# Folding landmark sums with shifted copies and VectorE additions, and loading the first k through SyncE, in a Nystrom attention plus feed-forward kernel

## The chip, the cores and the metric

The kernel runs on one core of a Trainium2 chip. The metric is device time in microseconds (us): the median of 12 runs before the change is 254.02 us, from 252.98 to 255.0. A core has five engines: TensorE (PE, matrix products; PEld is its weight load), VectorE (DVE), ScalarE (ACT), GpSimd (POOL) and SyncE (SP). They run their own instruction streams in order and meet through semaphores. SBUF is the on-chip memory with 128 partitions; PSUM holds what TensorE writes, in eight banks. Loads and stores are issued by SyncE or GpSimd and carried by 16 DMA engines.

## The reference

The reference is a Nystrom approximation of attention for 8 batches of 8 heads (576 tokens, 64 values a head), and a feed-forward layer on its output.

```python
q_lm = q.reshape(B, H, m, S // m, D).mean(axis=3)      # m = 32 landmarks, 18 tokens each
k_lm = k.reshape(B, H, m, S // m, D).mean(axis=3)
A  = sm(q, k_lm); Bm = sm(q_lm, k_lm); C = sm(q_lm, k) # softmax of scaled products
Z  = Bm.T / (norm1(Bm) * norminf(Bm) + 1e-6)
for _ in range(6):
    Z = 2 * Z - Z @ Bm @ Z                             # approximate inverse of Bm
attn = A @ Z @ C @ v                                   # per batch and head
h = attn_rows @ w_in                                   # 512 -> 2048
out = (relu(h) ** 2) @ w_out                           # 2048 -> 512
```

## The kernel before

**Attention.** For each batch, q and k are brought into a transposed form (`Ts`) in which a partition holds one of 64 values of a head for one of two parities of a token pair: partitions 0 to 63 the one, 64 to 127 the other. A landmark is a sum over 18 tokens. Summing along the free axis gives one partial sum for each parity (`parts["k"]` is the tile `kpart`, `parts["q"]` lies in `qpad`). The two parities must still be added. A *fold* does this on PE (line 681): a 128x128 matrix of four identity blocks times the partial sums puts into each half of the partitions the sum of both. For k the result is copied from PSUM into `kdup` (one copy of 128 x 256, line 686); for q into a block-diagonal tile `bdq` (two copies of 64 x 256, line 690). These copies go through the helper at lines 388 (ACT) and 390 (DVE).

`kdup` and the landmarks of q give the landmark scores (`b_mm`, lines 704 and 707); from them come the softmax and the inverse iteration, a chain of small steps that passes between PE and DVE (lines 869, 882 and 532 for the later batches; 732, 739 and 769 for batch 0). `bdq` and the transposed k give the scores C (line 917), whose exponentials (`EC`, line 924, ACT) are multiplied with v (lines 948 and 966). The product, normalised, meets the inverse (`Z4T`, `u`, `WT`), and `WT` times w_in gives `G` (line 1061). The softmaxed A is `AT`.

**Feed-forward.** `mlp_in` multiplies `AT` with `G` (line 1123 and the helper at 380), ACT takes the relu (1135), DVE squares it into `gT` (1138). `mlp_out` multiplies `gT` with w_out, 128 rows at a time, 16 matmuls of 512 columns each (1179); the result is copied from PSUM and stored by SyncE (1151), two pieces a tile. The very last tile is done in two cuts of columns, 0 to 256 and 256 to 512, each with its own copy and its own two stores.

**Batches.** The attention of batch b+1 is prepared while the feed-forward of batch b runs. Batches 0 and 1 get q and k in their transposed form by transposes on PE, with the landmark sums made on PE as well (lines 620, 630, 634); batches 2 to 7 get it by DMA transposes (548), and DVE sums (665, 668, 672).

**The order of the work.** Nothing runs in program order. Every operation is added to a plan (`Plan.add`) with the engine or engines that may do it, an assumed duration, what it reads and writes, the PSUM banks that it needs and a priority. `Plan.schedule` is a list scheduler: it takes the operation that can start earliest by its own model, critical ones first, then by priority. The choice between ACT and DVE for a copy (`either`) is made there too. The model has constants for latencies, for the DMA rate and for the delivery of PE's instructions in blocks of 256 (`BLOCK`, `AHEAD`, `FETCH`; idle warm-up matmuls and others count as `words`). `SHIFTS` is a packed table with one byte for each operation, which moves its priority, and `LOADS` does the same by hand for a few loads: in this kernel it exchanges v of batch 0 with the first quarter of w_in, and q with k of batch 1.

**The start.** SyncE loads heads 0 to 3 of k of batch 0 as float32 into the tile `kst`; ACT and DVE cast them into `kraw`, two heads each. GpSimd issues, in this order: the other half of k, both halves of q (these loads cast to bfloat16 on the way), the constants (`seg`, `ident`, `ones_f`), the first quarter of w_in, v, the second quarter of w_in, then q and k of batch 1, the rest of w_in and w_out. Meanwhile PE does 46 matmuls on zeros.

Of the kernel before, what the change touches and what calls it, by code (L numbers as in the profile page):

```python
# [9 lines left out]
P = 128  # L10
AF = mybir.ActivationFunctionType
ALU = mybir.AluOpType
# [3 lines left out]
F32 = mybir.dt.float32  # L16
# [18 lines left out]
LOADS = {11: 1.0, 12: -1.0, 14: 1.0, 15: -1.0, 20: 2.0, 22: -2.0}  # L35
SHIFTS = (
    "_kifEfPk#i`q#~XfPjF2fPjF2fPjFBw0!LK=GcTw3xm*acD7r)u|3E|?W>i|#1YHMcY%OszY04YG&)mLh+-9>?AvdR3UC<^KPWP&Mg0m*l0h"
    "_%bZcA%ZD+H0i~lW7WuJ&lPTK6G=)s#-*XVSf=zA4wOST1cgQj|u(lT}wNDPZtbZMf}#}gaUJs9OFG1t|~P}x1Of-_=LNTlOU#Fu&BK-ZgUn"
    "T$APhO|v`S3?L=76_~Y4F?~P6Df{V1EuXy4|%j;l_xzh0T@jMBZ&b4Fdri~B_9a^A2$I=JPIL5!)Y<Q69LhK4x5Sp0k^QE2R{J>RIy1aBr60"
    "EQqX6y41DQRp=tkZifyGII5;#z=XX7Bp1zTrkYmFhTqR=thl~G=%F5l1onpw>@ax+DYvuC))$H@w#PId9ykXkJaefgG;WOlWLk}ger@_<My7"  # L40
    "Hy+*z>ZQ{{Hs=^YAHFjFE4spYb+acmITS^T7Ux{(p@2I8C4S;_0{BbLjv2?ZE%Q$Bym4se<#6&yPRcMP9n8qm|KxE!#qTR4x@GMvGpp|H?z>"
    "FsX<CY0l7DZ+{wN7{YvU3W6(Fo+c(NbXnC%S0>IT@tn;Yl!`+-Z61DVUX>(Oaw2t7VJMIt(%j^>vH1A-&O9=<wvI@#lKlKX-~Ii;|0nnHs*C"
    "Sr)bY|^vEfE>>A<_q$J&9^)dlFYHS^HM=G@O~lZW@&^iaz3=dnx1@<0IrbDK7}v3xB)HAo6z0R|<s20-OLP5}=e8!Cfl1Trr^1b;0t1Tr`c4"
    "+P*lHdI^;SOh%;K}Q4xGztU-QxO_&#Va6^9SQ~0SKR^Gx>o7;b3GdfQch4(eoA1D7^(9~n>2euUgR7g6_*qgNCTcB6ee*o5vO?)lq(<sr~&M"
    "S7IFe;;<)$LKr7T7cM-k`Ty_nY2!ApE-mFM=;BEnncY4pNcUWjf1T_JmIs`&up3`6ax+DJsgyHpK<Il{VV7eTWX{@;G0sT#*(YjI8osh*NPW"
    "k%mxEN9{EgeD(KRY@wC|J$(K_3Ji0Z1(Y4hb7>511V$L;(doS1mLTPi`Af!YLjWtRy!90ZTMjO(z2u6sVPsHVBe5859@<J17knF989l0Rcl7"
    "z=#9~dIt~%SzVVvL|K;%lKjy~lbfg{QA|}&3Qm-aD=P`Q6wnPTy01u1j;?(L5WoKwKoAfi1hxe%0ggK$b#^d$R%Hh^Q9F#km~=K!0%jZn0#C"
    "AhjsX{7CLztImKO^dZ5{>;Rx@~+Bs+pe|0>OHz;W|Ul6aPMFCcj<1S_YFDg4c|>t?YS8Vu8bDFLK%I*$%~7h&^&ZX`2UgaQ-HBVPdl0gOddl"
    "%@n16bMngR0&i}WBXz#I2tFPLE5#N`u#TLrCi*C4e)jIJ7&3?g5|nwBGGz58mKRqATD`MK9%fdzmuMy#dBbIp#_-|cg%R|sD^@3X*pwp!f_N"
# [10 lines left out]

class Op:
    __slots__ = ("idx", "eng", "fn", "deps", "prio", "acq", "keys", "dma", "end", "grp", "fin", "mode",
                 "crit", "lead", "words", "pre", "fill")


class Plan:
# [1201 lines left out]
```

The softmax here doesn't subtract the row's maximum and nothing guards it: scores larger than these inputs give would overflow.

## Time and profile before

| what | value |
|---|---|
| median of 12 runs | 254.02 us |
| the profiled execution, its own time | 254.07 us |
| its span, first to last instruction | 252.4 us |
| PE busy | 243.3 us (96%) |
| DVE busy | 173.0 us (69%) |
| ACT busy | 164.5 us (65%) |
| fold matmuls (L681) | 16, two a batch |
| landing of k's SyncE half / GpSimd half | 5.0 / 7.6 us |
| landing of q's first / second half (batch 0) | 9.2 / 10.5 us |
| landing of w_in's first quarter / v (batch 0) | 13.3 / 16.9 us |
| first feed-forward matmul (L1123) | 24.1 us |
| last matmul ends / span ends | 248.5 / 252.4 us |

The span is counted from the first to the last instruction of the core; the rest of the execution's own time lies around it. In the rows of the profile, "L1179 PE" is line 1179 on TensorE. A row of a group of instructions gives the total busy time, the mean of one in ns, and after the bar the idle time of the engine ahead of them with what ended it. The chain that ended last is followed back from the last instruction to what released each step; its rows are start and length. "issue" is time in which an engine waited for nothing that the profile shows. Matmuls are pipelined, so the mean length of one (a latency) is longer than the distance from one to the next. In the DMA rows, a load that casts to bfloat16 is counted by the bytes that it writes, half of those that it reads.

### The profile page before, as it was taken

Reading aid. Unit: us, or ns where it says so; the run is one execution under the profiler, and the core shown is the slowest. Engines: PE = TensorE matmul, PEld = TensorE weight load, DVE = VectorE, ACT = ScalarE, POOL = GpSimd, SP = SyncE. Lnnn points to the kernel's source line nnn. Section 1 sums busy time; section 2 is a strip of 40 time slices with the busy share of each in tenths; the row PEclk is TensorE's granted clock in tenths of the full one; section 3 lists DMA queues with packets and bytes.
Section 4 is the critical chain, followed back from the end, with each engine's and each line's share of the span. In section 5 each row is a group of like instructions: output and inputs, shape, how many; then the busy total and the mean of one; then the engine's idle time right before and its main releaser. Section 6 shows DMA issues by size and latency. Waiting matters only on the chain.

```text
span 252.4 us, 6542 instructions
## 1 busy us (share of the span) xinstructions
PE 243.3 (96%) x2658; PEld 144.3 (57%) x2658; DVE 173.0 (69%) x479; ACT 164.5 (65%) x287; POOL 28.3 (11%) x51
## 2 busy tenths in 40 slices
PE   7787999999999999999999999999999999999993
PEld 7563874457654665466546565656554664466453
DVE  4655787869874999499699797987932756477000
ACT  3385998068773997388779987667814873388021
POOL 7822200003003000300210003001000000000000
PEclk9997999999999999999999999999999999999998
DMA  7999999999989999799599678999122203211123
GB/s 136 187 208 205 204 207 205 195 182 159 209 170 168 175 189 172 118 214 166 117 159 248 125 152 118 212 174 180 55 61 73 71 6 86 60 35 32 42 83 87
DMA packets 57055, 35.59 MB, mean 141 GB/s; under 512 B 29760, under 2 KB 52544, under 8 KB 57024
## 3 DMA queue, kind: packets, MB, share of 16 engines
q0 software_dynamic: 22672, 18.06, 47.9%
q1 hardware_dynamic: 34352, 17.11, 32.0%
q8 instruction: 21, 0.34, 0.5%
q14 instruction: 10, 0.08, 0.1%
HBM read 36.70 MB, written 9.44 MB: 183 GB/s over the span
## 4 chain that ended last, share of the span: by engine, by line
PE 90%; DMA 4%; POOL 2%; issue 1%; DVE 1%; ACT 0%; POOLq 0%; DVEq 0%
PE ps L1179 50%; PE ps L380 15%; PE ps L1123 13%; DMA vraw<-in_v_dram 4%; PE ps L1061 4%; PE ps L917 2%; PE ps L966 1%; PE ps L869 1%; PE ps L899 1%; PE ps L1006 1%; PE ps L681 1%; PE ps L707 1%; POOL qraw L456 1%; PE ps L948 0%; PE ps L560 0%
## 5 line engine op out<-in xcount | busy, mean ns | idle before, releaser
L1179 PE MATMUL ps<-w_out_bf,gT 128*128 128x512 bf16 (+1 forms) x592 | 144.8, 374 | 0.0
L1135 ACT ACTIVATE r<-ps 128x576 bf16<-128x576 f32 x128 | 76.3, 659 | 11.8 <-PE ps L380 10.2
L1179 PEld LDWEIGHTS <-gT 128*128 128x128 bf16 x592 | 53.5, 98 | 46.2 <-issue 5.7
L1138 DVE TENSOR_TENSOR gT<-r 128x576 bf16<-128x576 bf16 x128 | 55.7, 451 | 17.5 <-PE ps L1179 8.6
L1123 PE MATMUL ps<-AT,G 128*128 128x288 bf16 x256 | 66.3, 288 | 0.0
L380 PE MATMUL ps<-AT,G 128*128 128x288 bf16 x256 | 66.2, 287 | 0.0
L388 ACT COPY o<-ps 128x512 f32<-128x512 f32 (+1 forms) x30 | 17.0, 571 | 42.0 <-PE ps L1179 40.6
L380 PEld LDWEIGHTS <-G 128*128 128x128 bf16 x256 | 25.1, 98 | 10.6 <-issue 0.2
L1123 PEld LDWEIGHTS <-G 128*128 128x128 bf16 x256 | 25.1, 98 | 9.9 <-ACT G L388 0.8
L388 ACT CAST G<-ps 128x1024 bf16<-128x1024 f32 (+2 forms) x22 | 19.5, 939 | 5.6 <-PE ps L1061 5.5
L390 DVE CAST G<-ps 128x1024 bf16<-128x1024 f32 (+2 forms) x14 | 14.9, 1069 | 8.8 <-PE ps L1061 8.7
L882 DVE SCALAR_TENSOR_TENSOR st<-st,ps 128x128 bf16<-128x128 bf16 x35 | 9.9, 284 | 10.8 <-PE ps L869 10.8
L553 POOL COPY gate<-qT 1x1 bf16<-1x1 bf16 x6 | 1.2, 194 | 126.5 <-DMA qT<-qraw 107.2
L924 ACT ACTIVATE EC<-ps 96x512 bf16<-96x512 f32 x24 | 13.3, 604 | 0.5 <-PE ps L917 0.5
L869 PEld LDWEIGHTS <-Pd 128*128 128x128 bf16 x84 | 7.8, 97 | 8.5 <-DVE Pd L532 1.7
L532 DVE TENSOR_TENSOR Pd<-st,ones_d 128x256 bf16<-128x256 bf16 x42 | 12.1, 288 | 0.9
L1011 ACT ACTIVATE Ra<-ps 128x576 f32<-128x576 f32 x16 | 10.3, 652 | 3.5 <-PE ps L380 3.3
L1022 DVE TENSOR_TENSOR AT<-Ea,Ra 128x576 bf16<-128x576 bf16 x16 | 11.8, 751 | 0.3 <-ACT Ra L1015 0.3
L999 ACT ACTIVATE Ea<-ps 128x576 bf16<-128x576 f32 x16 | 9.8, 650 | 2.6 <-PE ps L899 2.6
L1061 PE MATMUL ps<-w_in_bf,WT 64*32 64x512 bf16 (+1 forms) x264 | 10.6, 390 | 0.0
L560 PE MATMUL ps<-zeros 128*128 128x128 bf16 (+2 forms) x52 | 6.8, 298 | 2.2 <-DVE zeros L482 1.3
L917 PEld LDWEIGHTS <-kT 128*128 128x128 bf16 x192 | 7.3, 98 | 2.6 <-issue 0.7
(156 smaller groups left out, 247.7 us busy)
## 6 DMA issues: line engine op xcount, KB each, us to landing
vraw<-in_v_dram POOLq DMA_DIRECT2D x8, 576.0 KB, 7.5
out_dram<-o SPq DMA_DIRECT2D x23, 192.0 KB, 2.6
qraw<-in_q_dram POOLq DMA_DIRECT2D x7, 576.0 KB, 13.3
kraw<-in_k_dram POOLq DMA_DIRECT2D x7, 576.0 KB, 11.1
out_dram<-o SPq DMA_DIRECT2D x24, 128.0 KB, 2.5
w_in_bf<-in_moe_w_in_dram POOLq DMA_DIRECT2D x4, 512.0 KB, 15.2
w_out_bf<-in_moe_w_out_dram POOLq DMA_DIRECT2D x4, 512.0 KB, 21.3
out_dram<-o SPq DMA_DIRECT2D x23, 64.0 KB, 2.3
```

Of the source, the lines that this page charges most:

```text
L380: nc.tensor.add_instruction(mybir.InstMatmult(start_tensor_calc=start, stop_tensor_calc=stop, is_transpose=transpose, ldweights=False, til ...
L388: nc.scalar.copy(dst, src)
L390: ENG[e].tensor_copy(dst, src)
L532: nc.vector.tensor_tensor(dst[:], src.unsqueeze(2).to_broadcast([P, 2, NG, M]), ones_d[:].unsqueeze(1).to_broadcast([P, 2, NG, M]), ALU.mult)
L917: nc.tensor.matmul(t[:, y, :], lhsT=Ts["k"][z][:, o:o + P], rhs=flat(bdq[:, h, :, :]), start=True, stop=True)
L924: nc.scalar.activation(EC[:, x, :, :, :, :].rearrange("p c i g m -> p (i g) c m"), PS[sc][0:TP, :, :].rearrange("p y (c m) -> p y c m", c= ...
L1022: add(("DVE", dve_ns(S)), lambda e, i=i: nc.vector.tensor_tensor(AT[:, i, :], Ea[:, i, :, :].rearrange("p c t -> p (c t)"), Ra[:, i, :, :] ...
L1061: nc.tensor.matmul(ts[i][M * g:M * g + M, lo:hi], lhsT=WT[64 * i:64 * i + 64, g, :], rhs=w_in_bf[64 * i:64 * i + 64, g, n * 512 + lo:n * 5 ...
L1123: (again if j else nc.tensor.matmul)(t[:, j, 0:HALF], lhsT=G[:, i, f * P:(f + 1) * P], rhs=AT[:, i, j * HALF:(j + 1) * HALF], start=(i == ...
L1135: add(("ACT", act_ns(S)), lambda e, hk=hk, r=r: nc.scalar.activation(r.rearrange("p (j t) -> p j t", j=2), PS[hk][:, :, 0:HALF], AF.Relu), ...
L1138: add(("DVE", dve_ns(S, 2)), lambda e, r=r, f=f: nc.vector.tensor_tensor(gT[:, f, z * S:z * S + S], r[:], r[:], ALU.mult), reads=[("r", rn ...
L1179: nc.tensor.matmul(PS[ok][:, 0:hi - lo], lhsT=gT[:, f, x0:x0 + P], rhs=w_out_bf[:, f, lo:hi], start=(f == f0), stop=(f == f1 - 1))
```

## The change

Four things are changed, and the table of shifts is a new one.

1. For batches 2 to 7 (`b > FOLD`) the fold matmul and the copies from PSUM go. The partial sums are copied into a second tile (`swaps`) with the two halves of the partitions exchanged, by two copies of 64 partitions on ACT or DVE, and DVE adds the two tiles: one addition into `kdup`, two of 64 partitions each into `bdq`.
2. All of k of batch 0 is loaded by SyncE as float32, in four loads of two heads, and cast by eight copies of one head each. Its transposes on PE run in four groups of six instead of two of twelve, with up to three filler matmuls each where PE would wait. GpSimd issues the first half of q, makes the constants, then issues the second half of q.
3. `LOADS` now exchanges the two parts of w_out in each pair, and no longer v with w_in, nor q with k. v of batch 0 is issued ahead of w_in.
4. The last tile is cut at column 384 in place of 256.

The planner's constants (DMA rate, time to landing, durations of issues, instruction delivery) are changed as well; they act on the order alone.

```diff
-LOADS = {11: 1.0, 12: -1.0, 14: 1.0, 15: -1.0, 20: 2.0, 22: -2.0}
+FOLD = 1
+LOADS = {26: 1.0, 27: -1.0, 29: 1.0, 30: -1.0}
...
-    DMA_NS_PER_BYTE = 1.0 / 410.0
+    DMA_NS_PER_BYTE = 1.0 / 401.0
...
-    BLOCK, AHEAD, FETCH = 256, 67, ((20000.0, 6000.0), (165000.0, 6800.0), (1e12, 4000.0))
+    BLOCK, AHEAD, FETCH = 256, 67, ((22000.0, 6400.0), (165000.0, 6800.0), (1e12, 4000.0))
...
-        dma_free = 2900.0
+        dma_free = 2150.0
...
+    swaps = {nm: sb.tile([P, NG, 2, M], BF16, name=nm + "sw") for nm in ("k", "q")}
...
-    kst = sb.tile([TP, H // 2, NC6 * D], F32, name="kst")
+    kst = sb.tile([TP, H, NC6 * D], F32, name="kst")
...
+            fine = not first or nm == "k"
...
-                n = 12 if first else 6
-                tag = "h" if first else "o"
+                n = 6 if fine else 12
+                tag = "o" if fine else "h"
...
+                        if n == 6:
+                            idle(bank(tp, [P, 512]))
...
+            if b > FOLD:
+
+                for x in range(2):
+                    add(either(256, 4), lambda e, x=x, part=parts[nm], sw=swaps[nm]: copy(
+                        e, sw[64 * x:64 * x + 64], part[64 - 64 * x:P - 64 * x]),
+                        reads=[(nm, "part", 0), (nm, "part", 1)], writes=[(nm, "sw", x)], prio=at(pk))
+                if nm == "k":
+                    add(("DVE", dve_ns(256, 2)), lambda e: nc.vector.tensor_tensor(
+                        kdup.rearrange("p (g i) m -> p g i m", i=2), parts["k"][:], swaps["k"][:], ALU.add),
+                        reads=[("k", "part", 0), ("k", "part", 1), ("k", "sw", 0), ("k", "sw", 1)], writes=["kdup"], prio=at(pk))
+                else:
+                    for i in range(2):
+                        r = slice(64 * i, 64 * i + 64)
+                        add(("DVE", dve_ns(256, 2)), lambda e, i=i, r=r: nc.vector.tensor_tensor(
+                            bdq[r, :, i, :].rearrange("p (g i) m -> p g i m", i=2), parts["q"][r], swaps["q"][r], ALU.add),
+                            reads=[("q", "part", 0), ("q", "part", 1), ("q", "sw", i)], writes=["bdq%d" % i],
+                            prio=at(pk + 0.05))
+                continue
...
-            cuts = [(0, 256), (256, 512)] if last else [(0, 512)]
+            cuts = [(0, 384), (384, 512)] if last else [(0, 512)]
...
-    def stage_k(e):
-        nc.sync.dma_start(kst.rearrange("p h (c d) -> p h c d", c=NC6),
-                          k[0, 0:H // 2].rearrange("h (p c) d -> p h c d", c=NC6))
-
-    add(("SP", 60.0), stage_k, writes=["kst"], dma=4.0 * (H // 2) * S * D, prio=-200.0, lead=1250.0)
-    load("k", 0, 2, (1,))
-    for x in range(2):
-        add(either(2 * NC6 * D), lambda e, x=x: copy(
-            e, raws["k"][0][:, 2 * x:2 * x + 2].rearrange("p h c d -> p h (c d)"), kst[:, 2 * x:2 * x + 2, :]),
-            reads=["kst"], writes=[("k", 0, 0, x)], prio=-100.0)
-    load("q", 0, 2)
+    for g in range(NG):
+        def stage_k(e, g=g):
+            nc.sync.dma_start(kst[:, 2 * g:2 * g + 2].rearrange("p h (c d) -> p h c d", c=NC6),
+                              k[0, 2 * g:2 * g + 2].rearrange("h (p c) d -> p h c d", c=NC6))
+
+        add(("SP", 500.0), stage_k, writes=[("kst", g)], dma=4.0 * 2 * S * D * 1.07, prio=-200.0 + g, lead=900.0,
+            land=520.0)
+        for x in range(2):
+            add(either(NC6 * D), lambda e, h=2 * g + x: copy(
+                e, raws["k"][0][:, h].rearrange("p c d -> p (c d)"), kst[:, h, :]),
+                reads=[("kst", g)], writes=[("k", 0, g, x)], prio=-100.0 + g)
+
+    def load_q(x):
+        hs = slice(4 * x, 4 * x + 4)
+        add(("POOL", 670.0), lambda e: nc.gpsimd.dma_start(
+            raws["q"][0][:, hs], q[0, hs].rearrange("h (p c) d -> p h c d", c=NC6)),
+            writes=[("q", 0, x)], dma=4.0 * 4 * S * D * 1.08, prio=ld(), lead=1300.0 - 500.0 * x, land=1150.0)
+
+    load_q(0)
     add(("POOL", 2200.0), constants, writes=["ident", "seg", "onesf"], prio=ld())
+    load_q(1)
```

## The prediction

> **What bounds the kernel now.** I read the page's busy times first, then the stage windows, then the chain that ended last, and for the two ends of the span the queues and the time line.
>
> ```profile
> span 252.4 us, 6542 instructions
> PE 243.3 (96%) x2658; PEld 144.3 (57%) x2658; DVE 173.0 (69%) x479; ACT 164.5 (65%) x287; POOL 28.3 (11%) x51
> ...
> 20.00:25.00 5.00, 4.22 (x61) 1.65 (x60) 2.60 (x6) 2.50 (x7) 1.37 (x2) 0.69 1.31 208
> ...
> 60.00:200.00 140.00, 139.88 (x1453) 80.88 (x1451) 110.31 (x295) 101.57 (x174) 10.93 (x18) 1.00 0.88 152
> ```
>
> The columns of a window are its length, then busy time of PE, weight loads, DVE, ACT and POOL, the granted clock, DMA share and GB/s. From 60 to 200 PE is never idle and DVE has 29.7 us free: there time is saved only by taking work off PE. From 20 to 25 the granted clock is 0.69.
>
> ```profile
> 6.52 10.42 DMA vraw<-in_v_dram
> 16.98 1.19 PE ps L948 x24
> ...
> 19.48 0.24 DVE Z4T L983
> ...
> 20.48 0.78 issue
> 21.25 0.19 PE ps L732 x3
> ```
>
> This is the chain (start, length): the start of the program, up to the first feed-forward matmul at 24.1, hangs on the landing of v at 16.94, then on small steps, then on 0.78 us in which PE has nothing to issue. Afterwards it is PE back to back until the last matmul ends at 248.53; 3.9 us of copy, store and closing follow.
>
> ```profile
> DMA packets 120, 0.18 MB, mean 369 GB/s; under 512 B 0, under 2 KB 120, under 8 KB 120
> ...
> q1 hardware_dynamic: 120, 0.18, 108.6%
> DMA packets 205, 0.15 MB, mean 151 GB/s; under 512 B 9, under 2 KB 205, under 8 KB 205
> ...
> q0 software_dynamic: 205, 0.15, 137.1%
> ```
>
> The DMA answers for 3 to 3.5 us (the SyncE load of half of k, f32 into f32) and 5 to 6 us (GpSimd loads, which write bf16, so 151 written is 302 read). The SyncE load moves its bytes faster than the GpSimd loads beside it.
>
> **1. No fold on PE for batches 2 to 7.** Twelve matmuls at L681 go. First a piece of the chain, then rows of groups (busy us, mean ns | idle before).
>
> ```profile
> 32.94 0.22 PE ps L681 x2
> ...
> L681 PE MATMUL ps<-kpart,fold 128*128 128x256 bf16 x8 | 2.2, 272 | 0.0
> L681 PE MATMUL ps<-qpad,fold 128*128 128x256 bf16 x8 | 2.2, 274 | 0.0
> L532 DVE TENSOR_TENSOR Pd<-st,ones_d 128x256 bf16<-128x256 bf16 x42 | 12.1, 288 | 0.9
> L390 DVE CAST kdup<-ps 128x256 bf16<-128x256 f32 x4 | 1.7, 419 | 0.9 <-PE ps L681 0.9
> ```
>
> The chain piece gives the pitch: two in 0.22 us, 0.11 each (272 is latency). 12 x 0.11 = -1.3 us, in stages where PE is the limit. It is 0 if PE waits in the freed slots, and little more than 1.3 at best.
>
> In exchange the copies of the folded sums from PSUM go. In these six batches DVE did three of kdup (0.42) and five of bdq (0.42), 3.4 us; ACT did three (0.39) and seven (0.37), 3.7 us. Added are 18 additions of 256 bf16 on DVE: by the L532 row, the same operation at that size, 0.288 each, 5.2 us. Added too are 24 shifted copies of 256 bf16 on 64 partitions, on either engine. No row has this form. The bounds are 0.19 (the 64-element cast at L826, 191 ns) and 0.42 (the PSUM cast); between them the 3072-element v copy (941 ns at L958) scales to about 0.22 on DVE if a fixed 0.15 is taken off first. I take 0.22 on DVE, or 0.37 on ACT. All on DVE: 5.2 + 5.3 - 3.4 = +7.1 us on DVE, -3.7 on ACT. All on ACT: +1.8 on DVE, +5.2 on ACT. I cost it at nothing: 7.1 us lie inside DVE's 29.7 idle and beside the previous batch's output matmuls. Without that cover it is up to +7.1. The adds wait for both copies, so behind them in DVE's order the squares into gT and the inverse iteration's steps wait; PE's weight loads wait for these now only 1.7 us (Pd) and 0.9 us (gT) in total.
>
> **2. The start.** All of k(0), four SyncE loads of two heads, replaces one SyncE load of four heads and a GpSimd load of the rest. Three SyncE issues are added (0.38 us each by the one at 0.81) and one GpSimd issue of 0.80 goes. SyncE has nothing else queued there. GpSimd now issues q's first half, makes the constants (2.31 us, 3.48 to 5.79 before), then issues q's second half.
>
> *Bytes.* Before, half of k was in by about 4.3 and q's last byte by about 9.9 (landing 10.5): 1.77 MB read in 5.6 us. After: 0.59 MB of k at 369 GB/s, 1.6 us, and 1.18 MB of q at about 0.36 MB/us read (the 7 to 10 us rows write 176 to 184 GB/s), 3.3 us: 4.9 us, or -0.7. At the 0.30 of the 5 to 6 us row it is -0.1; at the later 0.41 (w_in parts landing 2.5 us apart) -1.1. I take -0.7, the rate of the nearest time.
>
> The Trainium skill (DMA: Bandwidth & Descriptors, "Issuing engines are not separate DMA queues") speaks against this term: DMAs from any engine interleave on the same 16 DMA engines, and spreading them saves only sequencer issue time. By it this term is 0 and the sum ends 0.7 higher.
>
> *q's second half is issued later:* 4.35 in place of 2.82. The first GpSimd packet came about 2.4 us after its issue (1.37 to after 3.5), so these come by 6.8, when k and q's first half still fill the engines (to 7.5 at these rates). So 0; +1.5 if paid whole.
>
> *v goes ahead of w_in's first part* (the old order table exchanged them, the new one doesn't). v then lands at 9.2 + 2.9 + 0.65 = 12.7, not 16.94. Next late is the exponential of the scores, EC, done at 15.90: v's wait is worth up to 16.94 - 15.90 = 1.04. But the time line has a second gate. PE stalls on issue at 14.48 to 15.06 and 20.48 to 21.25, 6.2 us apart, and single 16 KB packets of the instruction queue start at 12.65, 18.85 and after 24.5, also 6.2 apart: PE's program comes in blocks, and arriving early only lengthens the second stall. Blocks move only as far as the words ahead of them are issued sooner, which follows k and q. I take half, -0.5 (ends 0 and -1.04, and -1.82 with the 0.78 stall gone too).
>
> The skill's Runtime: NRT & Kernel Launch, "Instruction fetch mechanics", has fetches in 16 KB blocks too, but calls the cost of a crossing mostly hidden. The trace's 0.78 us stall disagrees; by the rule v would be worth the whole 1.04, and the sum would end 0.5 lower.
>
> *Other edits here.* k's transposes in four groups of six: the 46 warm-up matmuls hold PE until 5.7 either way, so the first group gains nothing. The eight casts of 384 elements (two of 768 took 0.83 and 0.59) and two more kT copies run while ACT and DVE are idle: 0, at most +0.3 if the last cast is exposed. Up to nine filler matmuls run only where PE waits: 0, though their words use up blocks. w_in's first part lands near 15.3, ahead of its use at 23.1. The later parts, 1.6 to 1.9 us ahead of their use now, come 0.7 earlier for a use 1.2 earlier: about 1.1 of cover left, else that is the loss. w_out is reordered: its third part, now last, lands near 42.6 for a use near 43.4.
>
> Start together: -0.7 - 0.5 = -1.2 us (ends -2.5 and, with the late q, +0.8).
>
> **3. The end.** The last tile is cut at 384 in place of 256. PE does the same columns. The last copy shrinks from 0.37 to about 0.27 us. But the first cut's copy now ends some 0.35 us before the last matmul, not 1.35 before it, and SyncE issues four stores in a row:
>
> ```profile
> 247.20 1.80 SPq L1151 DMA_DIRECT2D out_dram<-o  x2
> ...
> 249.09 0.84 SPq L1151 DMA_DIRECT2D out_dram<-o  x2
> ```
>
> One at 0.53 and one at 1.22 in the first pair. With issues of 0.53 the last pair starts about 0.2 later after the last matmul than now; with a 1.22 again, 0.9. A gain is at most 0.1. I take +0.2.
>
> **4. The new order.** The table of shifts and the planner's constants give another order everywhere. No row prices it. In the chain after 30 us little but PE is listed, so it can give back at most about 1 us; a loss is bounded by nothing but the slack above. I take 0 and widen by 1.
>
> **Sum.** 254.07 (the profiled execution: span 252.4 and 1.67 around it; 0.05 above the median of 254.02) - 1.3 - 1.2 + 0.2 = 251.8 us; alone, this case spans 250.9 to 252.7.
>
> **Rivals.**
> - *The start gains it all* (250.5): the blocks move with the data, -2.5 in place of -1.2. For it: 1.04 plus 0.78 stand on the chain. Against: the fixed 6.2 us. 0.15.
> - *The start gains nothing* (253.0): same engines, same bytes, same blocks. For it: the 302 GB/s row. 0.15.
> - *Nor does the fold* (254.3): its slots turn into waits. For it: the freed 0.11 us slots are scattered. Against: no idle PE to hide in. 0.09.
> - *q's late issue is paid whole* (253.8): 254.07 - 1.3 + 0.8 + 0.2. Against: the DMA engines are busy then. 0.05.
> - *DVE becomes the bound* (slower): the additions stand ahead of the gT squares and the inverse iteration in batches 2 to 7. If half of the 7.1 us shows on PE, 251.8 + 3.55 = 255.4. It decides from about 3.0 us, 0.5 a batch (251.8 to 254.8). For it: DVE is 79% busy from 60 to 200 and in-order. Against: 29.7 us idle, and PE has output matmuls to do meanwhile. 0.17.
>
> **How the numbers follow.** The forecast has 0.39. A measurement of this kernel tells about 0.3%, 0.76 us, from no change. Faster holds the forecast and the first two rivals, 0.69; same the next two, 0.14; slower the last, 0.17. The range, 250.0 to 255.0, leaves out the far part of the slower case and the lowest part of the first rival, under 0.2 together.
>
> **What would show it.** L681 down to 4 matmuls; PE still full from 60 to 200, with DVE nearer 84% than 79%; waits of PE's weight loads on Pd and gT not above 3 us. v landing near 12.7 and no longer on the chain; q's second half landing near 9.8; the first feed-forward matmul (L1123) near 22.9 in place of 24.1; issue stalls still about 6.2 us apart. About 4.1 us from the last matmul to the end of the span. I am wrong if q's second half lands after 10.5, if the first block comes no earlier, or if PE shows gaps behind DVE after 60 us.

## The result: 255.75 us, 0.7% slower

The changed kernel takes 255.75 us (median of 12 runs, 254.23 to 256.46); the kernel before, on the same chip, 253.61. The ratio is 1.0072, with a 95% interval of 1.0049 to 1.0095. The forecast was 251.8 and the range ended at 255.0: wrong in its sign and outside its range.

The profiled execution took 255.71 us, with a span of 253.8 (254.07 and 252.4 before). Cut at the two events that the prediction used, the two profiled executions compare as follows.

| | before | after | difference | predicted |
|---|---|---|---|---|
| first feed-forward matmul | 24.11 | 26.25 | +2.14 | -1.2 |
| from it to the end of the last matmul | 224.41 | 223.58 | -0.83 | -1.3 |
| from there to the end of the span | 3.88 | 3.97 | +0.09 | +0.2 |
| around the span | 1.67 | 1.91 | +0.24 | 0 |

The sum is +1.64. The loss stands in the first 26 us.

### The profile after

The page's head, and stage windows (length, then busy time of PE, weight loads, DVE, ACT and POOL, the granted clock, DMA share, GB/s):

```profile
span 253.8 us, 6549 instructions
PE 244.8 (96%) x2648; PEld 143.9 (57%) x2648; DVE 178.5 (70%) x508; ACT 165.9 (65%) x290; POOL 27.6 (11%) x50
...
10.00:15.00 5.00, 4.62 (x82) 4.24 (x83) 1.71 (x3) 2.43 (x7) 1.49 (x2) 0.50 1.28 206
15.00:20.00 5.00, 4.99 (x97) 2.56 (x96) 3.12 (x18) 4.27 (x9) 1.53 (x2) 0.51 1.28 204
20.00:25.00 5.00, 4.41 (x126) 2.65 (x126) 3.63 (x15) 3.70 (x9) 1.28 (x2) 1.00 1.29 206
60.00:200.00 140.00, 139.81 (x1462) 80.29 (x1461) 118.06 (x327) 103.14 (x179) 11.04 (x18) 1.00 0.91 154
```

The first two of these windows in the kernel before:

```profile
10.00:15.00 5.00, 4.07 (x107) 2.70 (x104) 3.07 (x15) 4.02 (x10) 2.60 (x4) 1.00 1.27 204
15.00:20.00 5.00, 3.87 (x114) 2.73 (x113) 2.73 (x14) 3.69 (x9) 0.90 (x2) 1.00 1.28 206
```

From 60 to 200 PE is as full as before (139.81 of 140) with DVE at 118.06 of 140, the predicted 84%. What is new stands in the windows ahead of it: the granted clock is 0.50 for ten microseconds, from 10 to 20, where it was 1.00 before (there it fell to 0.69 from 20 to 25). This is not one unlucky execution: in every execution of the changed kernel the mean granted clock over the span was 0.976 to 0.987, while e9, e12 and e13 below each have executions at 1.0.

The chain that ended last (start, length) and, from PE's time line, the wait that opens it:

```profile
1.37 8.58 DMA qraw<-in_q_dram
...
12.13 0.64 ACT kT L393
12.77 0.30 ACT kpart L393
13.12 0.37 PE ps L709
...
26.25 0.30 PE ps L1151
```
```profile
9.99 0.21 PE L640 MATMUL ps<-seg,qraw 96*128 96x32 bf16 x1 [2.18 <-DMA qraw<-in_q_dram]
```

The path no longer opens with v, as predicted, but not for the predicted reason: v landed at 16.24, near the old 16.94 and not at 12.7. It is off the path because q's first half came late and all else moved back with it. That landed at 9.95, not 9.1 as before, PE stood idle for 2.18 us, and after that wait the clock was down. The landmark scores of batch 0 (line 732) start at 14.70; before they started at 11.47 (line 704). Between them and the feed-forward 1.1 us come back; the stalls on the blocks of PE's program (0.58 and 0.78 us before) are gone there.

The DMA answers for 7 to 8, 8 to 9 and 9 to 10 us (q1 is SyncE's queue, q0 GpSimd's; packets, MB, share of time):

```profile
q0 software_dynamic: 129, 0.10, 73.3%
q1 hardware_dynamic: 111, 0.15, 42.6%
...
q0 software_dynamic: 237, 0.18, 115.8%
q1 hardware_dynamic: 25, 0.04, 10.8%
...
q0 software_dynamic: 257, 0.19, 124.3%
q1 hardware_dynamic: 11, 0.02, 4.5%
```

This is the surprise of the case. SyncE's queue carries k alone, 4 x 288 KB, 1.18 MB. From 2 us on the one-microsecond answers give 0.20, 0.31, 0.14, 0.15, 0.16 and 0.15 MB: 1.11 MB, 94%, are in by 8.0. The last 6% trickle in for another 2.6 us: k's four loads land at 4.2, 5.2, 9.6 and 10.6. Nor was the total slow. Counting GpSimd's bytes twice (they are read as float32), 2.6 MB were read from 2 to 10 us, against 2.4 MB before. The bytes came as fast as I had reckoned; the loads did not land with them.

The fold and what replaced it (a line's view, then rows of groups: busy us, mean ns | idle before):

```profile
L709 PE MATMUL ps<-kpart,fold x2: 273/323/373, 13.1 to 32.3; 128*128 128x256 bf16 x2
L709 PE MATMUL ps<-qpad,fold x2: 273/334/394, 14.9 to 36.4; 128*128 128x256 bf16 x2
```
```profile
L700 DVE TENSOR_TENSOR bdq<-qpad,qsw 64x256 bf16<-64x256 bf16 x12 | 3.4, 284 | 0.2
...
L393 ACT COPY ksw<-kpart 64x256 bf16<-64x256 bf16 x6 | 2.4, 402 | 3.7 <-DVE kpart L682 3.6
L395 DVE COPY qsw<-qpad 64x256 bf16<-64x256 bf16 x9 | 2.0, 221 | 0.3
L694 DVE TENSOR_TENSOR kdup<-kpart,ksw 128x256 bf16<-128x256 bf16 x6 | 1.7, 284 | 0.0
```

Four folds are left, as predicted, and the prices taken from neighbouring rows hold: 284 ns an addition (0.288 assumed), 221 ns a shifted copy on DVE (0.22), 402 on ACT (0.37). DVE gained 5.5 us of work, under the bound of 7.1.

At the end of the span one row merges SyncE's last six stores: a pair from 247.26, and from 249.59 on the four of the last tile in a row, as foreseen, the last of them issued at 250.89:

```profile
247.26 4.04 SPq L1179 DMA_DIRECT2D out_dram<-o  x6
```

### The profile page after: what moved, and what is told of

Its sections match the earlier page's. It is cut to its first block, busy times and chain, and to the rows that moved or that the text cites. A ratio compares the mean times of both kernels' runs of the same rounds, so it can differ in the third digit from the quotient of the medians.

```text
span 253.8 us, 6549 instructions
## 1 busy us (share of the span) xinstructions
PE 244.8 (96%) x2648; PEld 143.9 (57%) x2648; DVE 178.5 (70%) x508; ACT 165.9 (65%) x290; POOL 27.6 (11%) x50
## 4 chain that ended last, share of the span: by engine, by line
PE 87%; DVE 5%; DMA 3%; ACT 2%; issue 1%; POOLq 0%
PE ps L1207 48%; PE ps L385 13%; PE ps L1151 11%; DMA qraw<-in_q_dram 3%; PE ps L1089 3%; PE ps L945 3%; DVE gT L1166 2%; PE ps L994 1%; PE ps L897 1%; PE ps L927 1%; ACT r L1163 1%; PE ps L1034 1%; DVE G L395 1%; PE ps L566 1%; DVE t L678 0%
## 5 line engine op out<-in xcount | busy, mean ns | idle before, releaser
L1207 PE MATMUL ps<-w_out_bf,gT 128*128 128x512 bf16 (+2 forms) x592 | 144.0, 374 | 0.1
L393 ACT COPY o<-ps 128x512 f32<-128x512 f32 (+2 forms) x31 | 17.7, 572 | 34.2 <-PE ps L1207 33.9
L395 DVE CAST G<-ps 128x1024 bf16<-128x1024 f32 (+2 forms) x15 | 15.9, 1076 | 2.9 <-PE ps L1089 2.9
L1039 ACT ACTIVATE Ra<-ps 128x576 f32<-128x576 f32 x16 | 10.2, 653 | 3.7 <-PE ps L385 3.5
L1089 PE MATMUL ps<-w_in_bf,WT 64*32 64x512 bf16 (+1 forms) x264 | 10.2, 375 | 0.0
L945 PEld LDWEIGHTS <-kT 128*128 128x128 bf16 x192 | 8.1, 102 | 2.5 <-issue 0.5
L945 PE MATMUL ps<-bdq,kT 128*128 128x64 bf16 x192 | 8.8, 199 | 0.2 <-DVE bdq L395 0.2
```

The lines of the kernel that those rows point to most:

```text
L393: nc.scalar.copy(dst, src)
L395: ENG[e].tensor_copy(dst, src)
L945: nc.tensor.matmul(t[:, y, :], lhsT=Ts["k"][z][:, o:o + P], rhs=flat(bdq[:, h, :, :]), start=True, stop=True)
L1089: nc.tensor.matmul(ts[i][M * g:M * g + M, lo:hi], lhsT=WT[64 * i:64 * i + 64, g, :], rhs=w_in_bf[64 * i:64 * i + 64, g, n * 512 + lo:n * 5 ...
L1207: nc.tensor.matmul(PS[ok][:, 0:hi - lo], lhsT=gT[:, f, x0:x0 + P], rhs=w_out_bf[:, f, lo:hi], start=(f == f0), stop=(f == f1 - 1))
```

## The experiments

Two theories stood at first. S: the loss is in the start, and the fold exchange gains as forecast. D: the fold exchange itself costs, through DVE. Later ones are named where they come up. All ratios are to the kernel before on the same chip, with 95% intervals.

**e1: the fold exchange alone, in the old order.** Where PE had its fold, ACT and DVE make the two shifted copies; where the sums were copied from PSUM, DVE adds, for batches 2 to 7. Every other instruction keeps its place.

```diff
             def fold_mm(e, part=part, fp=fp, sw=swaps[nm]):
+                if b > 1:
+                    copy("ACT", sw[0:64], part[64:P])
+                    copy("DVE", sw[64:P], part[0:64])
+                    return
...
-                add(either(256), lambda e, fp=fp: copy(e, kdup[:], PS[fp][:]), reads=[fp], writes=["kdup"],
+                add(either(256), lambda e, fp=fp: kdup_add(e) if b > 1 else copy(e, kdup[:], PS[fp][:]),
```

> The kernel before, its order kept, with the fold of batches 2 to 7 alone exchanged: at the place of the fold matmul stand the two shifted copies (one on ACT, one on DVE), at the place of the copies from PSUM the additions on DVE. Theory S (the start of the changed kernel costs the time, the fold gains): 0.8 to 1.3 us below before, PE still full from 60 to 200. Theory D (DVE becomes the bound): above before, up to 3 us, with PE waiting on DVE after 60 us. Theory O (the new order costs the time, not a part of the change): as S.

Measured: 258.11 us, ratio 1.0173 (1.0140 to 1.0205). The first feed-forward matmul came early, at 22.32, but from it to the last matmul it took 230.42 us, 6.0 more than before. The window from 60 to 200 us, and the longest wait of DVE:

```profile
60.00:200.00 140.00, 134.25 (x1374) 76.27 (x1403) 110.71 (x309) 99.00 (x170) 10.90 (x18) 1.00 0.88 152
```
```profile
DVE kdup L691 <- ACT ksw L388: 8.6, 3, 7.1
```

PE, which was never idle there, now is for 5.75 of 140 us, and DVE is no busier than before (110.71 against 110.31). An addition on DVE waits 8.6 us in three waits, once 7.1, for a shifted copy on ACT: the copy stands in ACT's order where PE used to do the fold promptly, and ACT is not there yet. This is D's direction, by another door: not DVE's capacity. That the position of the new steps in two in-order engines is the cause fits these waits, but is not shown: the longest one ends at 196 us, where PE is busy for 9.95 of 10 us, and PE's idle time is spread over the whole stretch.

**e2: the new start alone, in the old order.** The loads as changed, with the casts placed ahead of the transposes that need them.

```diff
-        nc.sync.dma_start(kst.rearrange("p h (c d) -> p h c d", c=NC6),
-                          k[0, 0:H // 2].rearrange("h (p c) d -> p h c d", c=NC6))
+        for g in range(NG):
+            nc.sync.dma_start(kst[:, 2 * g:2 * g + 2].rearrange("p h (c d) -> p h c d", c=NC6),
+                              k[0, 2 * g:2 * g + 2].rearrange("h (p c) d -> p h c d", c=NC6))
...
-    load("k", 0, 2, (1,))
```

> The kernel before, its order kept, with the loads of the changed kernel at the start alone: four SyncE loads for k of batch 0 with eight casts, and on GpSimd q's first half, the constants, q's second half; w_in's first part still ahead of v. Theory S: the last two parts of k land after 9 us, q's second half after 11, PE idles and its granted clock falls; first feed-forward matmul 1.0 to 2.5 us later than the 24.1 of before, time 1.0 to 2.5 us above before. Theory O: as before within 0.5 us.

Measured: 258.04 us, ratio 1.0165 (1.0118 to 1.0212), the first feed-forward matmul at 28.54, and 224.00 back to back after it. k's last part landed after 11 us here too (11.4), and since the old order takes all of k before q, PE waited for it twice:

```profile
10.13 0.19 PE L636 MATMUL ps<-seg,kraw 96*128 96x32 bf16 x1 [3.88 <-ACT kraw L394]
...
11.96 0.21 PE L636 MATMUL ps<-seg,kraw 96*128 96x32 bf16 x1 [1.24 <-ACT kraw L394]
```

So S holds for the start: the four loads land late with the old order behind them as with the new. The rest of S fell with e1.

**e3: v ahead of w_in, alone.**

```diff
-LOADS = {11: 1.0, 12: -1.0, 14: 1.0, 15: -1.0, 20: 2.0, 22: -2.0}
+LOADS = {14: 1.0, 15: -1.0, 20: 2.0, 22: -2.0}
```

> The kernel before with v of batch 0 issued ahead of w_in's first part alone (the planner then moves some steps between 12 and 22 us). v lands near 13.5 in place of 16.9. If the wait for v is worth its time: 0.5 to 1.0 us below before. If the blocks of PE's program decide: within 0.3 us of before, with a longer issue stall near 20.

Measured: 253.59 us, ratio 0.9991 (0.9967 to 1.0016). v landed at 14.4 in place of 16.9, and the first feed-forward matmul moved by 0.17, to 23.94. The half of the 1.04 that the prediction booked is not seen. But its reason, that the blocks of PE's program hold the start, is not borne out either: PE crosses both boundaries without a stall, and the longer one near 20 that was expected is not there. PE's last wait on DVE, and the windows from there to the first feed-forward matmul, in e3 and then in the kernel before:

```profile
18.75 0.48 PE L560 MATMUL ps<-zeros 128*128 128x384 bf16 x1 [1.10 <-DVE Y L801]
```
```profile
18.75:23.94 5.19, 4.83 (x68) 1.46 (x68) 2.26 (x7) 1.92 (x7) 1.53 (x2) 0.50 1.32 207
```
```profile
19.76:24.11 4.35, 3.57 (x57) 1.18 (x57) 2.41 (x7) 1.85 (x6) 1.53 (x2) 0.75 1.31 203
```

The stretch begins 1.01 us earlier, but takes 0.84 longer, though the one before has the 0.78 us stall in it. It runs at a clock of 0.50 throughout, and has 68 matmuls in place of 57, since the planner moved some small steps; what each of the two costs is not separated.

**e4: the changed kernel with PE kept busy while it waits for q.** Eleven more filler matmuls ahead of q's first half.

```diff
-                        warm(t[:, 0:P] if pairs else t, fill, pairs)
+                        warm(t[:, 0:P] if pairs else t, fill + (11 if fill == 3 else 0), pairs)
```

> The changed kernel, its order kept, with 11 more matmuls on zeros (512 columns, about 0.22 us each) where PE waits for q's first half. Theory S with the clock: granted clock above 0.9 from 10 to 20 us in place of 0.50, first feed-forward matmul at 25.3 or earlier in place of 26.25, time 0.8 to 1.5 us below the changed kernel, 0.0 to 0.4% above before. If the late landings alone cost the time: within 0.4 us of the changed kernel, 0.6 to 0.9% above before.

Measured: 256.28 us, ratio 1.0101 (1.0070 to 1.0132). The clock stayed at 1.00 to 22 us and the landmark scores came at 13.35, 1.35 earlier. It was all given back:

```profile
22.21 0.20 PE L760 MATMUL ps<-Y,Y 32*32 32x32 bf16 x4 [2.40 <-issue]
```

PE ran out of program for 2.40 us (the fillers themselves are 22 rows of it), the clock fell after that stall instead, and the first feed-forward matmul came at 26.67. So the halved clock alone is not the loss: with the clock kept up, the same time goes to a block of PE's program.

**e5: the fold exchange planned, with the old table.** The new operations go through the scheduler, and every old operation keeps its own shift.

```diff
-        end, log = self.schedule(self.shifts(len(self.ops)))
+        end, log = self.schedule(self.spread())
...
+            if b > 1:
...
+                for x in range(2):
+                    add(either(256, 4), lambda e, x=x, part=part, sw=swaps[nm]: copy(
```

> The kernel before with the fold of batches 2 to 7 exchanged as in the change, as operations of the plan (each takes the priority shift of the operation that it replaces), so that the planner orders the work around them; start, end and constants as before. If the loss of the run in the old order came from the place of the copies in the queues: 0.5 to 1.3 us below before. Theory D (the longer path through ACT and DVE costs, wherever it is put): 1 us or more above before.

Measured: 256.59 us, ratio 1.0102 (1.0063 to 1.0140). Start early (23.28), then 228.44 us to the last matmul, 4.0 more than before. Planning heals a third of e1's 6.0. What the other two thirds are, no run here separates; with the table that was made for it (e9, e12, e13) the exchange shows no such loss.

**e6: fewer rows of program.** e3 with a warm-up of 20 long fillers in place of 46 short ones, to bring the blocks' boundaries later in the work.

```diff
-                    fill = {("k", 0): 46, ("q", 0): 3}.get((nm, x0), 0) if first else 0
+                    fill = {("k", 0): 20, ("q", 0): 3}.get((nm, x0), 0) if first else 0
...
-                        warm(t[:, 0:P] if pairs else t, fill, pairs)
+                        warm(t, fill, pairs)
```

> The kernel before with v ahead of w_in and with the warm-up of 46 matmuls of 128 columns exchanged for 20 of 512 columns (about the same PE time), which takes 52 rows out of PE's program ahead of the first block boundary. Theory B (blocks of 256 rows, 6.2 us apart, hold the start): the issue stalls near 15 and 21 us shrink or go, first feed-forward matmul 0.5 to 1.2 us earlier than 24.1, time 0.4 to 1.2 us below before. If the number of rows does not matter: as the run with v alone, within 0.3 us of before.

Measured: 257.68 us, ratio 1.0144 (1.0109 to 1.0180). The boundary moved, but the first feed-forward matmul came at 25.21, and the part after it took 227.60, 3.2 more than before. The edit changes the model's words, so the scheduler gives another order under a table made for the old one. So it says nothing about blocks; that the 3.2 us are the price of that order is likely, as in e5, but not shown.

**e7: the four loads left alone on the DMA engines.** In the changed kernel GpSimd makes its constants first and reads one element of each part of k, so that its loads are issued when k is in.

```diff
+            if x == 0:
+                for g in range(NG):
+                    nc.gpsimd.tensor_copy(held[:], kst[0:1, 2 * g + 1, 0:1])
             nc.gpsimd.dma_start(raws["q"][0][:, hs], q[0, hs].rearrange("h (p c) d -> p h c d", c=NC6))
```

> The changed kernel with GpSimd making the constants first and issuing its loads only when all of k has landed. Theory C (k's last parts are late because GpSimd's queue runs beside SyncE's): all four parts of k land by 7.0 us. If four SyncE loads are slow by themselves: the last parts still land after 9 us. The time is longer than that of the changed kernel in both cases, since q comes later.

Measured, in one execution: 258.12 us (before: 253.76). q comes late, of course (first feed-forward matmul 28.57), but k's four loads now land by 7.3 in place of 10.6. The DMA answers for 4 to 5, 5 to 6 and 6 to 7 us:

```profile
q1 hardware_dynamic: 182, 0.26, 105.8%
...
q1 hardware_dynamic: 188, 0.26, 111.5%
...
q1 hardware_dynamic: 88, 0.11, 49.2%
```

7.3 is a little later than theory C's 7.0 and far from the rival's 9: four SyncE loads are not slow by themselves, they land late only beside GpSimd's queue. Also, alone, they move 0.26 MB a us, not the 0.369 that I had read from one half microsecond.

**e8 and e9: two loads of four heads in place of four of two.** The changed kernel otherwise.

```diff
-            nc.sync.dma_start(kst[:, 2 * g:2 * g + 2].rearrange("p h (c d) -> p h c d", c=NC6),
-                              k[0, 2 * g:2 * g + 2].rearrange("h (p c) d -> p h c d", c=NC6))
+            if g % 2 == 0:
+                nc.sync.dma_start(kst[:, 2 * g:2 * g + 4].rearrange("p h (c d) -> p h c d", c=NC6),
+                                  k[0, 2 * g:2 * g + 4].rearrange("h (p c) d -> p h c d", c=NC6))
```

> The changed kernel with k of batch 0 in two SyncE loads of four heads in place of four of two. Theory C: the last part lands after 9 us as with four. If the number of SyncE loads is the cause: the last part lands by 8.2 us.

> The changed kernel with k in two SyncE loads of four heads, now timed. Theory C (the number of SyncE loads beside GpSimd's queue decides when k lands, and with it the start): k lands near 5.3 and 7.5, the first feed-forward matmul near 24.4 in place of 26.25; with 223.6 back to back after it and 3.9 to the end the span is 251.9 to 252.7, so 0.2% below to 0.2% above the kernel before. Rival O (the new order of the whole kernel, not its start, is what costs): within 0.3% of the changed kernel, 0.4 to 1.0% above before.

Measured: e8, one execution, 254.62 us (before: 253.76); e9, timed, 253.34 us, ratio 0.9983 (0.9957 to 1.0010), against 1.0072 for the change. k lands at 5.4 and 7.6, q's halves at 8.7 and 10.2, the first feed-forward matmul is at 24.61 (24.38 in e8). So theory C as it stood for e8, after 9 us beside GpSimd's queue however many loads, is refuted, and its rival holds: it takes both, four loads and the queue beside them. The same bytes on the same queues, in two issues fewer, take back 0.9%. The DMA answers of e9 for 5 to 6, 6 to 7 and 7 to 8 us:

```profile
q1 hardware_dynamic: 166, 0.25, 108.8%
...
q0 software_dynamic: 121, 0.09, 59.6%
q1 hardware_dynamic: 103, 0.13, 57.6%
...
q0 software_dynamic: 272, 0.20, 131.4%
```

There is no tail: after 7 SyncE's queue has no packet left, and GpSimd's first packet comes only after 6, not at 4.0, though it is issued at the same 1.4. With four loads the two queues share the engines from 4.0 on, with two they run one behind the other. Why, no view here shows.

**e10: e9 with k's second half ahead of q on PE.** The transposes of k's groups 2 and 3 (with their casts and copies, listed in `early`) go ahead of those of q's first half (`q0`), as in the kernel before.

```diff
+        moved = [x for x in log if x[0] in self.early]
+        log = [x for x in log if x[0] not in self.early]
+        at = [x[0] for x in log].index(self.q0)
+        log[at:at] = moved
```

> As the last, and on PE the transposes of k's second half go ahead of those of q's first half, since they land earlier. Theory C: PE works on k's second half from about 7.5 to 8.5, waits for q until 8.8, and the landmark scores of batch 0 come 0.5 to 1 us earlier; row 192 of PE's program is issued earlier too, and the blocks with it: first feed-forward matmul 23.0 to 24.0, 0.2 to 0.6% below before. Rival B (the blocks come no earlier, since their fetches are behind the loads on the DMA engines): first feed-forward matmul as in the last kernel, 24.2 to 24.6, with a longer stall on issue ahead of it.

Measured: 254.42 us, ratio 1.0004 (0.9976 to 1.0033); first feed-forward matmul at 24.88, later than both theories had it. PE waited 1.07 us for the casts, the clock was 0.50 from 8.8 to 12.2, and three fillers that now stand between k and q took until 10.51 while q lay ready since 8.8. Its landmark scores (13.44) are later than e9's (12.17). The edit was clumsy; e13 repeats it better.

**e11: the changed kernel with the old loads.** Half of k by one SyncE load, the other half by GpSimd in bf16, both halves of q issued ahead of the constants.

```diff
+            if g == 0:
+                nc.sync.dma_start(kst[:, 0:4].rearrange("p h (c d) -> p h c d", c=NC6),
+                                  k[0, 0:4].rearrange("h (p c) d -> p h c d", c=NC6))
+            if g == 2:
+                nc.gpsimd.dma_start(raws["k"][0][:, 4:8], k[0, 4:8].rearrange("h (p c) d -> p h c d", c=NC6))
```

> The changed kernel with the loads of the start as they were before: heads 0 to 3 of k by one SyncE load, heads 4 to 7 by GpSimd in bf16, both halves of q issued ahead of the constants; the order table, the fold exchange and the rest as changed. Theory C: the four SyncE loads were the whole loss, and the rest of the change is a gain: k lands at 5.0 and 7.6, q at 9.2 and 10.5, first feed-forward matmul 23.9 to 24.6, span 251.4 to 252.2, 0.1 to 0.4% below before. Rival O: the loss stays, 0.4 to 1.0% above before.

Measured: 253.88 us, ratio 1.0020 (0.9991 to 1.0049): between the two theories. k's second half is in at 8.0 (7.6 before), yet the first feed-forward matmul is at 25.55. PE's time line shows the rest of the loss:

```profile
9.38 0.19 PE L649 MATMUL ps<-seg,qraw 96*128 96x32 bf16 x1 [1.49 <-DMA qraw<-in_q_dram]
...
11.78 0.27 PE L718 MATMUL ps<-kpart,fold 128*128 128x256 bf16 x1 [0.60 <-ACT kpart L402]
...
16.32 0.22 PE L954 MATMUL ps<-bdq,kT 128*128 128x64 bf16 x2 [0.52 <-issue]
...
22.51 0.21 PE L769 MATMUL ps<-cvb,Z4T 32*32 32x64 bf16 x4 [1.34 <-issue]
```

The new order puts q's first half ahead of k's second half on PE. So PE waits 1.49 us for q while k lies ready, does k's second half after it, then waits 0.60 for kpart on ACT; the scores come at 12.79 in place of 11.47, and both stalls on the blocks come later too (16.32 and 22.51 in place of 15.06 and 21.25).

**e12: e11 with k's second half ahead of q on PE.** e10's edit on e11.

> The kernel of the last experiment (changed table, fold exchange and end, with the loads of the start as before), and on PE the transposes of k's second half go back ahead of those of q's first half, where the kernel before has them; its kpart then is ready before q's second half lands. Theory T (what is left of the loss with the old loads is the new table's order of the first 15 us on PE): landmark scores at 11.3 to 11.6 in place of 12.79, the stalls on issue end at 15.0 to 15.2 and 21.2 to 21.4 as before the change, first feed-forward matmul 23.9 to 24.4, and with 223.6 to 224.0 back to back and 3.6 to 3.9 after it a span of 251.1 to 252.3: 0 to 0.5% below before. Rival F (the fold exchange and the rest gain nothing at all): 0.1 to 0.4% above before, as the last one.

Measured: 252.42 us, ratio 0.9943 (0.9914 to 0.9972). This is the side of theory T: scores at 11.49 as it had them; the first feed-forward matmul at 23.86 and the span, 250.8, just below its bounds; only one stall is left, to 20.13, not two to 15.0 and 21.2. The kernel is faster than the one before and the changed one: it is the changed kernel with its new loads taken back, and with one pair of groups back in their old place on PE. From the first feed-forward matmul it is 223.30 us to the last matmul, and 3.64 to the end. PE's time line around the change, and the stall that is left:

```profile
10.34 0.27 PE L729 MATMUL ps<-kpart,fold 128*128 128x256 bf16 x1 [0.30 <-ACT qpad L407]
...
20.13 0.21 PE L780 MATMUL ps<-cvb,Z4T 32*32 32x64 bf16 x4 [0.76 <-issue]
```

**e13: e10 with its fillers moved ahead of k's second half.**

```diff
+                        if fill == 3:
+                            return
...
+        next(x[0] for x in moved if "PE" in x[0].eng).fill = 3
```

> Two SyncE loads of four heads, k's second half ahead of q on PE as in e10, with the three filler matmuls moved from between k's second half and q to ahead of k's second half, where PE waits. Theory B (the blocks of PE's program set the start): the clock stays at 1.00 from 5 to 15 us, q's transposes start at 9.2, landmark scores 11.1 to 11.4 (12.17 with the table's order, 13.44 in e10), then the stall ahead of row 448 or 704 grows, and the first feed-forward matmul comes at 24.0 to 24.6, 0.1 to 0.5% below before. Rival (data sets it): first feed-forward matmul near 23.5, 0.5% or more below before.

Measured: 253.24 us, ratio 0.9988 (0.9955 to 1.0022). Clock 1.00 from 5 to 15, scores at 11.49, a 0.98 us stall to 20.36, the first feed-forward matmul at 23.38: earlier than in any kernel that was timed here with the new order, e12 among them. Yet it is not faster than e9 beyond the intervals, and its part behind, 224.58, is longer than e12's 223.30. So the first feed-forward matmul is where the rival (data sets the start) had it, and the time is not.

Where an earlier start goes, the traces show in part. e8 and e9, one kernel, differ in the part behind by 1.16 us (224.74 and 223.58). The windows from the first feed-forward matmul to the ninth, e8 above, e9 below:

```profile
24.38:26.92 2.54, 2.54 (x29) 1.80 (x22) 0.27 (x1) 2.23 (x4) 0.79 (x1) 0.50 1.22 201
```
```profile
24.61:26.01 1.40, 1.40 (x28) 1.20 (x21) 0.28 (x1) 1.40 (x3) 0.79 (x1) 1.00 1.21 199
```

The same work takes 1.14 longer at a clock of 0.50, and the two stay 1.16 apart to the end. So the part behind depends also on whether a stretch of low clock, which begins in the small steps ahead of the first feed-forward matmul, is over when that starts. In e9 and e12 it is (at 24.46 and 23.67); in e8 it lasts to 26.95, in e13 to 24.88, 1.51 us too long. By the ninth feed-forward matmul e13 is 0.72 behind e12; the other 0.56 of their 1.28 stand later and are left open.

## Why the prediction was wrong, step by step

**The step that failed is the bytes of the start (-0.7).** It divided bytes by a rate and took the quotient for a landing. The bytes were right: 2.6 MB by 10 us, against 2.4 before. But a load lands when its last piece lands. With four SyncE loads beside GpSimd's queue the last 6% of k took 2.6 us, and q, predicted complete at 9.8, landed at 12.0 (9.95 for its first half). The condition that the text set for itself, q's second half after 10.5, was met, and so was the second: the first fetch of a block started at 13.8, not 12.7. e9 shows the size: with the same bytes in two loads the first feed-forward matmul comes 1.64 us earlier than with four, and the time is 0.9% shorter. Even then q is complete at 10.2, not 9.8: 0.3 ahead of the 10.5 of before, not 0.7. The rate itself, 0.369, was one half microsecond at the head of a load; e7 has 0.26 over its length.

The Trainium skill has a reason that would give such a gap (DMA: Bandwidth & Descriptors, "Why a DMA increments its semaphore by 16 and not by 1"): a DMA runs on up to 16 engines that finish independently, and its semaphore is full only when the last has delivered. The trace agrees with it as far as it goes, 94% by 8.0 and the landing at 10.6; whether and which of the engines were behind, no view here shows.

The section that the prediction weighed against this term ("Issuing engines are not separate DMA queues") was the better guide: by it moving k to SyncE saves only issue time. But by it the term would be 0, and what came with four loads was a loss.

**The second failure is part 4, the new order (0, give or take 1).** e11 to e12 is one pair of k's groups ahead of or behind q's first half on PE, a place set by the order alone: 1.0020 to 0.9943, and 25.55 to 23.86 at the first feed-forward matmul. That is 1.7 us, more than the 1 by which the range was widened. In the changed kernel itself the two failures cannot be added up: there k's second half landed at 9.6 and 10.6, beside q's first half at 9.95, and what the order alone cost is not shown. The prediction looked for what an order can give in the steady part, where PE is full, and not at the start, where it is idle.

**q's second half issued later (0, up to 1.5):** no loss is seen where k does not trail. With two SyncE loads and the late issue at 4.2 (e9) it lands at 10.2; before the change, issued at 2.8, at 10.5.

**v ahead of w_in (-0.5):** nothing that can be measured (e3). The reason given against it, that arriving early only lengthens the second stall on a block, is not what e3 shows: the stalls are gone, and the gain goes in a stretch of other order at a clock of 0.50 (from 18.6 to 25.4; 21.9 to 25.3 before). v's landing, predicted at 12.7, was 16.2 in the changed kernel, 14.4 in e3 and 13.1 in e9, where k does not trail.

**Other edits of the start at 0:** PE did wait for the new casts, 0.91 us to 6.19 in e9 and 1.07 us to 8.27 in e10, but no run prices them alone. The filler matmuls did not keep the clock up in the 2.18 us for which q was late, and no term of the sum stood for a change of the clock.

**The fold off PE (-1.3):** mis-sized. The pair of profiles says -0.83, but part of that is the clock: of the part behind the first feed-forward matmul 1.21 us (to 25.32) ran at 0.50 in the kernel before, and none in the changed one. If half of such a stretch is lost, an estimate that gives 1.28 for e8 against the 1.16 measured, that is 0.6 of the 0.83. Over all traces, the part is 223.3 to 224.7 with the new order (nine traces, mean 223.88) and 224.0 to 224.8 with the old one (three, mean 224.39). With half of each low stretch taken off, the means are 223.5 and 223.9: -0.4 by estimate, a third of -1.3, and the new order and the other edits are in it. No run has the exchange alone in an order made for it, so what twelve matmuls less are worth is not shown. e12, whose loads and order of the start are near the old ones, is 0.57% faster in all, 1.4 us. Among executions whose mean granted clock was 0.999 or more, its spans are 249.7 to 250.8 us (five), and those of the kernel before on that chip 250.4 to 251.5 (four, an outlier of 1377 left out). That the exchange can cost in an order that was not made for it was not in the prediction: in the old order it costs 6.0 us (e1), planned with the old shifts 4.0 (e5).

**DVE becomes the bound (rival, slower, 0.17):** did not happen in the changed kernel; PE is full from 60 to 200. In e1 and e5 PE did lose time after 60 us (busy 134.25 and 135.74 of 140), though DVE was busy for 110.71 and 113.72, less than the 118.06 of the changed kernel: not by DVE's busy time.

**The end (+0.2):** +0.09 in the pair, but nothing can be told from it: from the last matmul to the end it is 3.6 to 4.0 us in the nine traces with the new cut, and in those with the old one 3.6 to 3.9, with one of 5.0 (e2).

## What to carry to other kernels

A load's landing is not its bytes over a rate: when two queues share the engines, look at the tail of each queue, microsecond by microsecond, and try fewer and larger loads before changing who issues them. When a change brings a new order table, compare the order of the first steps on the engine that waits there with the order in which their data land; one misplaced pair of groups cost more here (1.7 us at the first feed-forward matmul) than the whole part behind it gained. An exchange of instructions between engines is not to be judged inside an order that was made for the old ones. And before a difference between two profiles is put down to an edit, compare the granted clock in the same stretch: here it made 1.16 us between two executions of one kernel.

## What the runs showed of the hardware

- Four SyncE loads of 288 KB beside GpSimd's queue land last at 10.6 us; two of 576 KB at 7.6; four alone at 7.3.
- PE's program comes in blocks of 256 rows: where two stalls on issue stand in one trace, 128 matmuls and 128 weight loads lie between them (15.06 to 21.25 before, 16.32 to 22.51 in e11, 6.2 us apart in both). In the eight kernels with a stall of over 0.5 us at the second boundary it ended 2.3 to 2.5 us after the start of a 16 KB packet of the instruction queue: 18.90 to 21.25 (before), 20.06 to 22.51 (e11), 17.84 to 20.13 (e12).
- After PE had been idle for 2.18 us, to 9.99, the granted clock was 0.50 from 9.6 to 19.9, ten microseconds in which PE was 73% to 100% busy in every one. In the first 30 us of the traces (e1 has none) the low stretches have three lengths, one, two or three times 3.4 us: 3.4 in the kernel before (from 21.9), e4, e5, e9, e10 (twice), e11, e12 and e13; 6.8 in e3, e6 and e8; 10.2 in the changed kernel, e2 and e7. The Trainium skill (TensorE: Matmul & The Clock Gate, section Part 1: The HAM clock gate, the "warmup" mystery) has the clock come back after at least one busy window of about 3.4 us. The lengths agree with that; what kept the clock down through three of them in the changed kernel, no run here shows.
